# A fused attention and token-mixing kernel: a new static order of its instructions (measured durations, a reserve of buffers, PSUM emptied first, squares into later buffers, GpSimd products by chunks)

## The chip, the cores and the metric

The kernel runs on one core of one Trainium2 chip. A core has five engines that run at the same time, each through its own list of instructions in a fixed order: PE (TensorE, the matrix unit), DVE (VectorE), ACT (ScalarE), POOL (GpSimd) and SP (SyncE, which here only starts transfers). They wait for each other through semaphores. SBUF is the working memory, PSUM the eight banks into which PE writes; 128 partitions each.

The metric is the device time of one execution in microseconds (us), the median of several runs. The profile describes one further execution of the same program; its span, from the first to the last instruction, is a little shorter than the measured time.

## The reference

Two blocks follow each other. The first is an attention with a polynomial feature map; the second mixes tokens. There are 4 batches, 4 heads, 1088 positions, and 4 x 32 = 128 channels.

```python
def phi(x):                                   # r = 8 features from each of two sketches, 64 products
    a = einsum('rd,bhsd->bhsr', S1, x)
    b = einsum('rd,bhsd->bhsr', S2, x)
    return einsum('bhsi,bhsj->bhsij', a, b).reshape(..., r * r)
q_p, k_p = phi(q), phi(k)
kv  = einsum('bhsf,bhsd->bhfd', k_p, v)       # sums over all positions
z   = sum(k_p, axis=2)
num = einsum('bhsf,bhfd->bhsd', q_p, kv)
den = einsum('bhsf,bhf->bhs', q_p, z)[..., None] + 1e-06
x   = (num / den) as (batch, seq, 128)

theta = x @ w_theta
zr, zi = x * cos(theta), x * sin(theta)
y = einsum('ts,bsd->btd', w_tok_r, zr) + einsum('ts,bsd->btd', w_tok_i, zi)   # 1088 x 1088 each
u = x + y
return u + maximum(u @ w_ch, 0)
```

The token weights come in 64-bit floating point, so the kernel first makes 32-bit rows out of them. The denominator can come near zero, so it is computed with numbers split into a coarse and a fine part.

## The kernel before

The kernel doesn't write its instructions in the order in which they run. It records operations (`op`) with the engine, an estimated duration, and the buffers that they read and write. `Layout.run` then orders all of them when the program is built: it repeats "which ready operation can start first, and of those within a small slack, which is due first", keeps account of when engines and buffers come free, and fixes both the order on each engine and which buffer each value gets. On the chip nothing is decided any more.

```python
LAT = {"P": 0.16, "V": 0.12, "A": 0.12, "G": 0.16, "S": 0.10}
HURRY = 100.0
SLACK = {"P": 0.05, "V": 0.25, "A": 0.25, "G": 0.25, "S": 0.4}
...
def run(self):
    ... # due of an operation: the earliest due of those after it, less their duration and the latency
    for o in ops:
        if o.eng in "VA" and any(b.cls == "ps" for b in o.bufs):
            o.due -= self.HURRY                        # what empties PSUM goes first
    ...
    def place(o, strict=True):                         # is there room for the buffers of o, and from when
        ...
            k = len(bs) + (max(b.keep for b in bs) if strict else 0)
            if len(av) < k:
                return None
    ...
        t, o = min((c for c in cand if c[0] <= first + self.SLACK[e]), key=lambda c: (c[1].due, c[1].i))
...
classes = {"big": (24, 1152), "zs": (5, 2176), "lv": (1, 5 * NT), "hf": (2, 576), "g3": (4, 768),
           "g1": (4, 384), "sm": (12, 192), "ps": (5, 512), "py": (3, 512)}      # buffers, words each
```

The work, in the order of the data. "Row" is one of the 17 slices of the token weights (128 positions of the real or the imaginary part, the last one 64 of each).

```python
def weight(dst, dfn, src, n):                  # one 64-bit row into 32 bits
    raw = buf("zs", (n,), I64, "raw", cap=3)
    stp = buf("big", (n, 2), I16, "step", keep=0, cap=2)
    op("S", n * 1024 / 250e3, lambda: SY.dma_start(raw(), src), ...)
    op("A", 0.2 + n * 0.0009,  lambda: A.activation(dfn(), <high words>, AF.Copy, scale=2.0**-112), ...)
    op("A", 0.2 + n * 0.00105, lambda: A.activation(<step, upper half>, <high words>, AF.Copy, scale=2.0**-60), ...)
    op("A", 0.2 + n * 0.00105, lambda: A.activation(<step, lower half>, <low words>, AF.Copy, scale=2.0**-29), ...)
    op("V", n * 0.00095 + 0.05, lambda: ts(dfn(), dfn(), 3, ALU.logical_shift_left), ...)
    op("V", n * 0.0012 + 0.08, lambda: tt(V, dfn(), dfn(), stp(), ALU.add), ...)

def key_sums(b):                               # exact sums over the keys, for the denominator
    junk = buf("big", ...)
    op("A", ..., lambda: A.activation(junk(), kx(), AF.Square, accum_out=km()[:, 2:3]), ...)
    ...                                        # DVE: coarse part, rest, fine part
    op("G", pool_(n), lambda: tt(G, r(), r(), kb()[:, :, 1], ALU.subtract), [r], [(kb, 1)])
    tps = kfeatures(b)
    vop(n, lambda: stt(kc(), r(), -0.5, kc(), ALU.mult, ALU.add), [kx], [r])
    for c in range(NC):
        op("P", 0.4, lambda c=c: sums(c), [t], [kb, r, kx])      # 9 chunks
    ...

def kfeatures(b):                              # features of the keys, 3 groups, and k_p x v
    for g in range(NG):
        ...                                    # PE transposes, ACT, PE features, ACT
        op("G", pool_(CH * R * R), lambda: tt(G, kp(), <a>, <b>, ALU.mult), [kp], [ks])    # 128 x 768
        op("P", 1.0, sums, [acc], [kp, vx])

def chain(bs): ...                             # small matrices from the sums: PE and DVE by turns; for (0,) and (1, 2, 3)
def query_scale(b): ...                        # ACT squares of q into a "junk" buffer, PE, DVE
def query_slices(b): ...                       # PE transposes of q, ACT, DVE: coarse half and rest
def levels(b): ...                             # PE, ACT, then some 13 DVE operations: q features and 1/den

def outputs_x(b, lv, pool_qp):                 # 3 groups of 384 positions
    ...                                        # products q_p (DVE for batch 0, POOL for 1 to 3), PE transposes, ACT,
                                               # PE num, ACT, PE theta, ACT/DVE: cos and sin, DVE: z = x*cos, x*sin

def mix_row(b, i, gs, yps, due): ...           # PE: y += z[:, i] x row i; for batch 0 all three groups per row
def mix_out(b, g, yp, due): ...                # u, u @ w_ch, relu, out
...
due0, per = 40, 3.0
t = due0
for b in range(B):
    lv = levels(b)
    outputs_x(b, lv, b > 0)
    gss = ((0, 1, 2),) if b == 0 else tuple((g,) for g in range(NG))
    for gs in gss:
        for i in range(NK):
            t += per if b == 0 else 0.65
            mix_row(b, i, gs, yps, t)
        for g, yp in zip(gs, yps):
            mix_out(b, g, yp, t + 6.0)
```

Batch 0 is mixed row by row while the rows are still being made; batches 1 to 3 use all 17 finished rows, which stay in SBUF.

Of the kernel before, what the change touches and what calls it, by code (L numbers as in the profile page):

```python
# [21 lines left out]
P = 128  # L22
# [5 lines left out]
UP = 256.0  # L28
QFIX = 2.006
# [3 lines left out]
class Buf:  # L33


    def __init__(self, cls, shape, dt, name, keep=0, cap=99):
        self.cls, self.shape, self.dt, self.name, self.keep, self.cap = cls, shape, dt, name, keep, cap
        self.ops, self.left, self.slot, self.ap, self.end = [], 0, None, None, 0.0
# [5 lines left out]
class Op:  # L44
    __slots__ = ("eng", "dur", "fn", "bufs", "pred", "succ", "due", "wait", "ready", "start", "end", "i")


class Layout:
# [3 lines left out]
    HURRY = 100.0  # L52
    SLACK = {"P": 0.05, "V": 0.25, "A": 0.25, "G": 0.25, "S": 0.4}
# [5 lines left out]
    def buf(self, cls, shape, dt, name, keep=0, cap=99):  # L59
        return Buf(cls, shape, dt, name, keep, cap)  # L60

    def op(self, eng, dur, fn, w=(), r=(), due=None, hold=()):
        o = Op()
        o.i, o.eng, o.dur, o.fn, o.due = len(self.ops), eng, dur, fn, 1e9 if due is None else due
        o.succ, pred = [], set()
# [41 lines left out]
    def run(self):  # L107
        ops = self.ops
        for o in reversed(ops):
            for s in o.succ:  # L110
                t = ops[s]
                lat = 0.0 if t.eng == o.eng else self.LAT[o.eng]
                if o.eng == "S":
                    lat += 2.0
                o.due = min(o.due, t.due - t.dur - lat)
            o.wait, o.ready = len(o.pred), 0.0
        for o in ops:
            if o.eng in "VA" and any(b.cls == "ps" for b in o.bufs):
                o.due -= self.HURRY
# [6 lines left out]
        def place(o, strict=True):  # L126
# [5 lines left out]
            for c, bs in need.items():  # L132
                av = sorted(s[0] for s in slots[c] if s[1] is None)
                if any(sum(s[1] is not None and s[1].name == b.name for s in slots[c]) >= b.cap for b in bs):
                    return None
                k = len(bs) + (max(b.keep for b in bs) if strict else 0)
                if len(av) < k:
                    return None
# [3 lines left out]
        while done < len(ops):  # L142
            pick = None
            for e in "PVAGS":
                cand = []
                for o in ready[e]:
                    t = max(free[e], o.ready)
# [7 lines left out]
                t, o = min((c for c in cand if c[0] <= first + self.SLACK[e]), key=lambda c: (c[1].due, c[1].i))  # L155
                if pick is None or t < pick[0]:
                    pick = (t, o)
            if pick is None:
                loose = [(o.due, o.i, o) for e in "PVAGS" for o in ready[e] if place(o, False) is not None]
                if loose:  # L160
                    o = min(loose)[2]
                    pick = (max(free[o.eng], o.ready, place(o, False)), o)
            if pick is None:
                raise RuntimeError("no room: " + str([(o.eng, [b.name for b in o.bufs]) for e in "PVAGS" for o in ready[e]][:9]) + str({c: [x[1] and x[1].name for x in v] for c, v in slots.items()}))
            t, o = pick
            e = o.eng
            for b in o.bufs:
                if b.slot is None and b.cls is not None:
                    s = min((x for x in slots[b.cls] if x[1] is None), key=lambda x: x[0])
                    s[1], b.slot = b, s  # L170
            o.start = t
# [60 lines left out]
def pool_(n):  # L232
    return 0.06 + 0.0021 * n
# [3 lines left out]
def kernel(  # L237
# [30 lines left out]
        "hf": (2, 576),  # L268
        "g3": (4, 768),
# [86 lines left out]
    if wide:  # L356
# [24 lines left out]
        op("V", 1.1, unpack, [(sp, 0), y, z], [st])  # L381
# [52 lines left out]
    op("V", 1.2, scaled, [ab, sc, s0, sf, sq], [sp, pw])  # L434
# [89 lines left out]
    def weight(dst, dfn, src, n):  # L524
        if src.dtype == F32:
            op("S", n * 512 / 250e3, lambda: SY.dma_start(dfn(), src), [dst], [])
            return
        raw = buf("zs", (n,), I64, "raw", cap=3)
        stp = buf("big", (n, 2), I16, "step", keep=0, cap=2)
        op("S", n * 1024 / 250e3, lambda: SY.dma_start(raw(), src), [raw], [])  # L530
        op("A", 0.2 + n * 0.0009, lambda: A.activation(dfn(), words_of(raw(), n)[1].bitcast(F32), AF.Copy,  # L531
                                                     scale=2.0**-112), [dst], [raw])
        op("A", 0.2 + n * 0.00105, lambda: A.activation(stp()[:, :, 1].bitcast(F16), words_of(raw(), n)[1].bitcast(F32),  # L533
                                                     AF.Copy, scale=2.0**-60), [(stp, 1)], [raw])
        op("A", 0.2 + n * 0.00105, lambda: A.activation(stp()[:, :, 0], words_of(raw(), n)[0].bitcast(U32), AF.Copy,  # L535
                                                     scale=2.0**-29), [(stp, 0)], [raw])
        op("V", n * 0.00095 + 0.05, lambda: ts(dfn().bitcast(I32), dfn().bitcast(I32), 3, ALU.logical_shift_left),
           [dst], [])
        op("V", n * 0.0012 + 0.08, lambda: tt(V, dfn().bitcast(I32), dfn().bitcast(I32),
                                          stp().rearrange("p n t -> p (n t)").bitcast(I32), ALU.add), [dst], [stp])  # L540
# [4 lines left out]
    def load(b, nm, due=None):  # L545
        src = {"k": k, "q": q, "v": v}[nm]
        t = ld[nm, b] = buf("big", (NC, H, D), F32, f"{nm}{b}", keep=5)
        op("S", 576 * 1024 / 250e3, lambda: SY.dma_start(t().rearrange("p c h d -> p (c h d)"),
                                                        src[b].rearrange("p c h d -> p (c h d)")), [t], [], due)
# [4 lines left out]
    def key_sums(b):  # L554
# [6 lines left out]
        junk = buf("big", (NC * HD,), F32, "junk")  # L561
        op("A", act(n) + 0.1, lambda: A.activation(junk(), kx().rearrange("p c h d -> p (c h d)"), AF.Square,
                                                   accum_out=km()[:, 2:3]), [junk, (km, 1)], [kx])
        kg[b] = fixed((2,), F32, f"kg{b}")
        pg = buf("ps", (512,), F32, "pg", keep=2 * (b > 0))
# [14 lines left out]
        vop(n, lambda: rnd(kb()[:, :, 0], kc(), km()[:, 0:1]), [(kb, 0)], [kx, (km, 0)])  # L580
        vop(n, lambda: tt(V, r(), kc(), kb()[:, :, 0], ALU.subtract), [r], [kx, (kb, 0)])
        vop(n, lambda: rnd(kb()[:, :, 1], r(), km()[:, 1:2]), [(kb, 1)], [r, (km, 0)])
        op("G", pool_(n), lambda: tt(G, r(), r(), kb()[:, :, 1], ALU.subtract), [r], [(kb, 1)])
        tps = kfeatures(b)
        vop(n, lambda: stt(kc(), r(), -0.5, kc(), ALU.mult, ALU.add), [kx], [r])
# [457 lines left out]
```

## Time and profile before

| what | value |
|---|---|
| time, median of 3 runs (lowest, highest) | 298.12 us (297.23, 298.13) |
| span of the profiled execution, and its own time | 292.5 us, 294.28 us |
| PE busy | 253.1 us, 87% of the span |
| DVE busy | 166.6 us, 57% |
| ACT busy | 143.3 us, 49% |
| POOL busy | 61.2 us, 21% |
| read from and written to memory | 26.30 MB and 2.23 MB |

In the profile a line of a group names the line of the program, the engine, the operation, the buffers written and read by their class (`big`, `zs`, `ps` and so on, as in `classes` above) and the shape. Matmuls into `py` are the token mixing; a 32-bit matmul shows as two records. A busy engine can be held up inside an instruction: the length of one instruction against the usual length of its group tells that. Busy time is listed for PE as records that overlap, so it is best read beside the work itself.

### The profile page before, as it was taken

What the parts mean: (1) busy time and instruction counts of PE and PEld (TensorE: products, weight loads), DVE (VectorE), ACT (ScalarE), POOL (GpSimd) and SP (SyncE); (2) the same over time, 40 slices, a digit from 0 to 9 for tenths busy, and PEclk for the clock granted to TensorE, in tenths of its full rate; (3) what the DMA queues carried; (4) which work ended last, traced back from release to release, by engine and by line L of the source; (5) the groups of instructions that cost most, each with busy time, mean ns of one, the idle gap of its engine ahead of it and who ended that gap; (6) DMA issues with size and microseconds to landing.
All of it is one profiled execution on the core that took longest, in us unless ns stands there. A gap on an engine that the chain in (4) does not pass through costs nothing.

```text
span 292.5 us, 3825 instructions
## 1 busy us (share of the span) xinstructions
PE 253.1 (87%) x1447; PEld 183.3 (63%) x1447; DVE 166.6 (57%) x343; ACT 143.3 (49%) x231; POOL 61.2 (21%) x67
## 2 busy tenths in 40 slices
PE   2329969677979999999199999999999999999993
PEld 2329859454557878867067667676657676666671
DVE  2998787998996966799985304813400721501001
ACT  5454945869886988999048202037300235500000
POOL 0328912502371307200270000140000060000000
PEclk9999968979999999999689999999999999999999
DMA  6999910040564457620001101000001010000000
GB/s 214 411 417 420 415 46 3 0 152 2 173 262 160 147 195 272 205 117 2 0 0 30 51 0 29 0 27 0 2 22 27 0 29 0 0 25 7 20 27 24
DMA packets 9155, 28.77 MB, mean 98 GB/s; under 512 B 945, under 2 KB 5297, under 8 KB 6961
## 3 DMA queue, kind: packets, MB, share of 16 engines
q1 hardware_dynamic: 9136, 28.53, 26.7%
q8 instruction: 11, 0.18, 0.2%
q14 instruction: 8, 0.06, 0.1%
HBM read 26.30 MB, written 2.23 MB: 98 GB/s over the span
## 4 chain that ended last, share of the span: by engine, by line
PE 64%; DVE 17%; ACT 11%; DMA 4%; issue 3%; SPq 0%; DVEq 0%; ACTq 0%
PE py L311 37%; PE ps L311 22%; DVE big L295 4%; DMA zs<-w_tok 3%; ACT big L531 3%; DVE lv L295 3%; ACT big L533 2%; ACT big L535 2%; DVE big L299 2%; PE ps L863 2%; DVE big L302 1%; DMA big<-k_l 1%; DVE g L295 1%; PE ps L948 1%; DVE sm L295 1%
## 5 line engine op out<-in xcount | busy, mean ns | idle before, releaser
L311 PE MATMUL py<-big,zs 128*128 128x384 f32 (+1 forms) x408 | 137.1, 477 | 8.4 <-DVE big L295 7.1
L311 PEld LDWEIGHTS py<-big,zs 128*128 128x128 f32 x408 | 73.8, 192 | 50.5 <-DVE big L295 8.9
L958 ACT ACTIVATE g<-ps 128x384 f32<-128x384 f32 (+2 forms) x16 | 6.1, 406 | 77.0 <-PE ps L311 77.0
L295 POOL TENSOR_TENSOR g<-lv 128x768 f32<-128x768 f32 x9 | 15.9, 1789 | 100.5 <-DVE lv L295 100.5
L295 POOL TENSOR_TENSOR g<-sm 128x768 f32<-128x768 f32 x12 | 24.5, 2045 | 39.9 <-ACT sm L630 29.2
L295 DVE CUSTOM_DVE_ANT_0 big<-big,big 128x2176 uint16<-128x2176 uint16 x17 | 24.3, 1430 | 6.5 <-ACT big L535 5.8
L533 ACT ACTIVATE big<-zs 128x1088 f16<-128x1088 f32 (+1 forms) x18 | 24.8, 1380 | 0.0
L535 ACT ACTIVATE big<-zs 128x1088 int16<-128x1088 uint32 (+1 forms) x18 | 24.7, 1372 | 0.0
L295 DVE TENSOR_TENSOR g<-big,py 128x384 f32<-128x384 f32 (+1 forms) x12 | 6.2, 527 | 31.1 <-PE py L311 31.1
L295 DVE TENSOR_TENSOR g<-g,ps 128x384 f32<-128x384 f32 (+2 forms) x16 | 6.9, 450 | 26.4 <-PE ps L948 19.3
L531 ACT ACTIVATE big<-zs 128x1088 f32<-128x1088 f32 x17 | 20.4, 1201 | 0.0
L302 DVE SCALAR_TENSOR_TENSOR g<-g,ps 128x384 f32<-128x384 f32 x12 | 6.6, 553 | 22.4 <-ACT g L893 22.4
L311 PE MATMUL ps<-big,big 128*128 128x128 f32 x72 | 16.8, 317 | 1.2 <-DVE big L302 1.2
L867 ACT COPY g<-ps 128x384 f32<-128x384 f32 x24 | 10.4, 488 | 14.9 <-PE ps L863 14.8
L299 DVE TENSOR_SCALAR big<-big 128x1088 int32<-128x1088 int32 x17 | 17.0, 1003 | 1.3 <-ACT big L531 1.3
L295 POOL TENSOR_TENSOR big<-big,big 128x1152 f32<-128x1152 f32 x4 | 10.4, 2608 | 31.1 <-DVE big L299 26.9
L311 PE MATMUL ps<-mf,big 128*128 128x96 f32 x72 | 16.0, 320 | 0.0
L295 DVE TENSOR_TENSOR zs<-ps,g 128x768 f32<-128x768 f32 (+2 forms) x20 | 12.3, 629 | 3.3 <-ACT g L899 3.3
L863 PE MATMUL ps<-ident,g 128*128 128x128 f32 x72 | 11.1, 299 | 3.4 <-DVE sm L299 3.4
L311 PE MATMUL ps<-mv,hf 128*128 128x96 f16 x108 | 12.0, 218 | 2.0 <-DVE mv L299 1.1
L863 PEld LDWEIGHTS ps<-ident,g 128*128 128x128 f32 x72 | 9.2, 154 | 6.2 <-issue 4.8
L311 PEld LDWEIGHTS ps<-big,big 128*128 128x128 f32 x72 | 11.6, 202 | 2.1 <-DVE big L302 1.6
(159 smaller groups left out, 393.9 us busy)
## 6 DMA issues: line engine op xcount, KB each, us to landing
zs<-w_tok SPq DMA_DIRECT2D x17, 1088.0 KB, 5.0
big<-k_l SPq DMA_DIRECT2D x4, 576.0 KB, 10.1
big<-q_l SPq DMA_DIRECT2D x4, 576.0 KB, 12.6
big<-v_l SPq DMA_DIRECT2D x4, 576.0 KB, 12.9
out<-g SPq DMA_DIRECT2D x8, 192.0 KB, 2.1
out<-g SPq DMA_DIRECT2D x4, 128.0 KB, 1.8
zs<-w_sq SPq DMA_DIRECT2D x1, 256.0 KB, 4.9
out<-g SPq DMA_DIRECT2D x4, 32.0 KB, 1.8
```

The lines of the kernel that those rows point to most:

```text
L295: eng.tensor_tensor(out=o, in0=a, in1=b, op=f)
L299: (eng or V).tensor_scalar(out=o, in0=a, scalar1=s1, scalar2=s2, op0=op0, **kw)
L302: (eng or V).scalar_tensor_tensor(out=o, in0=a, scalar=s, in1=b, op0=op0, op1=op1)
L311: T.matmul(o, lhs, rhs, start=start, stop=stop, skip_group_check=True)
L531: op("A", 0.2 + n * 0.0009, lambda: A.activation(dfn(), words_of(raw(), n)[1].bitcast(F32), AF.Copy, scale=2.0**-112), [dst], [raw])
L533: op("A", 0.2 + n * 0.00105, lambda: A.activation(stp()[:, :, 1].bitcast(F16), words_of(raw(), n)[1].bitcast(F32), AF.Copy, scale=2.0**-60 ...
L535: op("A", 0.2 + n * 0.00105, lambda: A.activation(stp()[:, :, 0], words_of(raw(), n)[0].bitcast(U32), AF.Copy, scale=2.0**-29), [(stp, 0)] ...
L863: T.transpose(tr()[:, i * P:(i + 1) * P], qp()[:, i * H + 2 * n:i * H + 2 * n + 2].rearrange("p h i j -> p (h i j)"), ident())
L867: op("A", act(GW), lambda n=n, tr=tr, qT=qT: A.copy(qT()[:, n], tr()), [(qT, n)], [tr])
L948: T.transpose(un()[:sz, i * P:(i + 1) * P], uT()[:, i * P:i * P + sz], ident())
L958: op("A", act(m), lambda n=n, i0=i0, i1=i1, o=o: A.activation(o(), po()[:n, i0 * P:i1 * P], AF.Relu), [(ot, j)], [po])
```

## The change

The order on all engines is made anew. Nothing of the arithmetic changes: each engine executes the same operations as before, except that each large POOL product is now three smaller ones. The parts:

- **Durations of the trace.** The estimates given to `op` are replaced by lengths that a trace showed (for instance small DVE chains 2.5 us instead of 1.1, feature matmuls 0.615 instead of 0.67, loads at 380 to 400 GB/s instead of 250).
- **A reserve of buffers for what is due first.** The fixed `keep` and `cap` of each buffer go. A buffer that is due later may only be taken while enough free ones remain for those due earlier, up to `RESERVE` of its class.
- **PSUM emptied first.** The 100 us of hurry for what empties PSUM now changes only the choice among ready operations (`rank`), no longer the due time (`due`), which the reserve and the new lead times use.
- **Squares into later buffers.** The squares that only serve their sum are written where a later value will stand (`kb`, `qx`), not into a buffer of their own; the half-corrected keys get their own buffer `kh`, so the keys aren't overwritten.
- **POOL products by chunks.** Each product of 128x768 becomes three of 128x256, each difference of 128x1152 three of 128x384.
- **Due times and lead times.** Rows are due at 55.2 + 2.18 i us of the layout's own clock, mixing at 54.7 + 2.05 per row; loads of q, k and v may start at most 40 us ahead of their due time. One more buffer in `hf` and `g3`.

```diff
+MIX = (54.7, 2.05, 0.691, 0.0)
+ROWS = (55.2, 2.18)
+LOAD_LEAD = 40.0
+RAW_LEAD = 1000.0
+CHAINS = ((0,), (1, 2, 3))
+QPOOL = (False, True, True, True)
...
+    RESERVE = {"big": 8, "zs": 2, "lv": 0, "hf": 1, "g3": 3, "g1": 2, "sm": 4, "ps": 3, "py": 0}
...
-            o.wait, o.ready = len(o.pred), 0.0
+            o.wait, o.ready, o.rank = len(o.pred), 0.0, o.due
         for o in ops:
             if o.eng in "VA" and any(b.cls == "ps" for b in o.bufs):
-                o.due -= self.HURRY
+                o.rank -= self.HURRY
...
-                k = len(bs) + (max(b.keep for b in bs) if strict else 0)
-                if len(av) < k:
+                last = max((b.due, b.ops[0]) for b in bs)
+                before = bisect.bisect_left(pending[c], last, key=lambda x: x[:2]) - len(bs) + 1
+                if len(av) < len(bs) + min(max(before, 0), self.RESERVE[c]):
                     return None
...
-                    t = max(free[e], o.ready)
+                    t = max(free[e], o.ready, o.due - o.lead)
...
-        "hf": (2, 576),
-        "g3": (4, 768),
+        "hf": (3, 576),
+        "g3": (5, 768),
...
-        junk = buf("big", (NC * HD,), F32, "junk")
-        op("A", act(n) + 0.1, lambda: A.activation(junk(), kx()..., AF.Square, accum_out=km()[:, 2:3]), [junk, (km, 1)], [kx])
+        op("A", act(n) + 0.1, lambda: A.activation(kb()[:, :, 0], kx()..., AF.Square, accum_out=km()[:, 2:3]), [(kb, 0), (km, 1)], [kx])
...
-        op("G", pool_(n), lambda: tt(G, r(), r(), kb()[:, :, 1], ALU.subtract), [r], [(kb, 1)])
+        def rest():
+            for g in range(NG):
+                x = r()[:, g * GC:(g + 1) * GC]
+                tt(G, x, x, kb()[:, g * GC:(g + 1) * GC, 1], ALU.subtract)
+
+        op("G", pool_(n) + 0.1, rest, [r], [(kb, 1)])
         tps = kfeatures(b)
-        vop(n, lambda: stt(kc(), r(), -0.5, kc(), ALU.mult, ALU.add), [kx], [r])
+        kh = buf("big", (NC, HD), F32, "kh")
+        vop(n, lambda: stt(kh(), r(), -0.5, kc(), ALU.mult, ALU.add), [kh], [r, kx])
...
+            def outer(kp=kp, ks=ks):
+                for i in range(GC):
+                    h = slice(i * H, (i + 1) * H)
+                    tt(G, kp()[:, h], bc(ks()[:, h, 0:R], ...), bc(ks()[:, h, R:2 * R], ...), ALU.mult)
...
-    due0, per = 40, 3.0
-    t = due0
+    t = MIX[0]
...
-                t += per if b == 0 else 0.65
+                t += MIX[1] if b == 0 else MIX[2]
...
-                mix_out(b, g, yp, t + 6.0)
+                mix_out(b, g, yp, t + 6.0 + (3.0 * g if b == 0 else 0.0))
```

## Prediction

> **What bounds the kernel now.** I began with the page's picture of 40 slices (7.3 us each, busy share in tenths), to see in which stretches PE has holes.
>
> ```profile
> PE   2329969677979999999199999999999999999993
> ...
> DVE  2998787998996966799985304813400721501001
> ACT  5454945869886988999048202037300235500000
> POOL 0328912502371307200270000140000060000000
> ```
>
> PE is sparse to slice 8 and has one hole in slice 19; after it PE is full to the end while DVE and ACT are half idle. So there are stages. I cut the trace at the first transposes of query products (60 us), at the end of batch 0's mixing (149) and at the last matmul (288.2), and asked for busy time in each stretch (PE, weight loads, DVE, ACT, POOL, then clock, DMA share, GB/s):
>
> ```profile
> 0.00:60.00 60.00, 38.03 (x287) 33.95 (x287) 47.68 (x142) 35.06 (x60) 24.60 (x49) 0.94 0.62 242
> 60.00:149.00 89.00, 77.00 (x485) 56.76 (x486) 75.89 (x116) 70.09 (x86) 25.27 (x12) 0.94 0.37 134
> 149.00:288.20 139.20, 138.06 (x678) 92.56 (x675) 42.41 (x85) 38.04 (x85) 11.29 (x7) 1.00 0.06 16
> 288.20:292.50 4.30, 0.00 (x0) 0.00 (x0) 0.61 (x2) 0.06 (x1) 0.00 (x0) 0.91 0.15 40
> ```
>
> The third stage is PE alone, 138.06 of 139.2 us. The second has PE, DVE and ACT all at 79 to 87%: no engine is full, they wait for each other. The waits of PE name the largest of these:
>
> ```profile
> PE py L311 <- DVE big L295: 7.1, 3, 6.1
> PE ps L393 <- DVE m L411: 5.9, 1, 5.9
> PE ps L619 <- DMA big<-k_l: 4.7, 1, 4.7
> PE ps L863 <- DVE sm L299: 3.4, 1, 3.4
> PE ps L311 <- DVE psc L495: 3.2, 1, 3.2
> ```
>
> The 6.1 us is the hole in slice 19: the last weight row waits on DVE, which has the whole levels chain of batch 1 (138.0 to 144.2 us) ahead of the row's last step. The others lie in the first 21 us and before batch 0's products. Last, why DVE is slow there; the timeline of DVE, then of POOL, in one window:
>
> ```profile
> 78.02 0.71 DVE L299 TENSOR_SCALAR big<-big 128x1088 int32<-128x1088 int32 x1
> ...
> 81.23 2.90 DVE L299 TENSOR_SCALAR big<-big 128x1088 int32<-128x1088 int32 x1
> ```
>
> ```profile
> 80.24 3.31 POOL L295 TENSOR_TENSOR big<-big,big 128x1152 f32<-128x1152 f32 x1 [4.16 <-issue]
> ```
>
> The same shift takes 0.71 us alone and 2.90 us when POOL has begun a long difference just before; it ends as soon as POOL has (83.55).
>
> [...]2.2 us lost in one hold. Other such excesses over the usual length in the second stage: 1.9 (74.05 us), 1.3 (85.33), 1.3 (97.97), 1.2 (114.40), 1.3 and 1.2 (145.38, 147.48): about 10 us with the 2.2. [...]Here a 128x32 product takes 0.21 us and an undisturbed 128x768 one 1.48, which makes 1.73 ns per element and 0.155 us fixed[...]. [...]a chunk of the levels matmuls takes 0.75 us at 42 us and 0.39 from 46 us; the row at 145.5, behind the hole, takes 3.50 instead of 1.9.[...]
>
> **The yardstick.** All PE work, by start-to-start spacings where PE is dense: mixing 136 x 0.645 + 68 x 0.54 = 124.4; 220 transposes x 0.11 = 24.2; levels 36 x 0.39 = 14.0; key sums 36 x 0.445 = 16.0; key features 36 x 0.205 = 7.4; k_p v 72 x 0.134 = 9.6; num 24 x 0.40 = 9.6; theta and the last product 72 x 0.222 = 16.0; folding 16 x 0.22 = 3.5; small ones 6.1. Sum 230.8 us. The change leaves it as it is; it can only alter how much is lost beside it. Before, the work done at the two cuts is 26.6 and 96.2, so the stages lost 60 - 26.6 = 33.4, 89 - 69.6 = 19.4 and 139.2 - 134.6 = 4.6 us.
>
> **First stage.** From the recorded order of the changed kernel, walked by hand with the old trace's lengths:
> - The five small sketch loads now go before k. Five issues at about 0.45 us put k about 2.3 us later: landing 6.9 instead of 4.5. That is a loss. In exchange DVE unpacks the sketches while it waits for k, not after it behind a 2.36 us hold.
> - Coarse and fine parts of k on DVE end near 13.0 (before 11.8), POOL's rest near 15.5. The sketch scaling starts at 16.0 (18.2 before) and ends 17.7. The half-corrected keys follow at once, 17.7 to 19.0; before they came after all small pieces, 24.0 to 26.4, also held by POOL.
> - So batch 0's key sums start at 19.0 instead of 26.15. From there to the end of the levels matmuls the old kernel took 21.3 us; I give the new one 24, because two k_p v sums stand ahead of the levels on PE and wait for POOL products, and DVE takes q's rest (1.35) only after the small chain. The levels end at 43, not 47.5.
> - From the levels to the first query transposes: 12.6 us before, of which some 3.6 were POOL holds (this DVE chain takes 9.8 us in batch 0, 6.2 in batch 1). I take 10.5.
> Together 53.5 us instead of 60. PE has done 24.3 of its work by then, 2.3 less than before.
>
> **Second stage.** PE has 96.1 - 24.3 = 71.8 us to do. The three other limits, summed along the new order with the old durations less their 0.08 to 0.11 us overlap: ACT from the first copies of query products to the last row's conversion 65.4 us; DVE from there to the last row's addition 66.6 us (16 shifts at 0.64, 17 additions at 1.22, levels 6.2, chain 4.65, and so on), with perhaps 6 of holds 73. PE, ACT and DVE would be done within 8 us of each other, so PE leads narrowly. What is new in the order: the 27 key-sum chunks of batches 1 to 3 (12 us) lie around the first mixed rows, where PE used to wait for z and rows, and the levels chain of batch 1 comes when the seventeenth row is five rows away. The 6.1 us hole and its 1.6 us of slow clock go. I take 71.8, 2.5 of overhead as in the dense stage (4.6 / 134.6), 3 of slow clock after the thin start, 3 of waits: 80 instead of 89.
>
> **Third stage and end.** The same instructions, 134.7 + 4.6 = 139.3, and 4.3 for the last copies and transfer, which aren't touched.
>
> **Chunks alone.** Each product costs 2 x 0.155 = 0.31 us more on POOL, 25 of them some 8 us: POOL from 61 to about 69 busy, nearly all beside other work. A hold can last 0.6 to 0.8 us instead of 1.5 to 2.4.
>
> **Sum.** 53.5 + 80 + 139.3 + 4.3 = 277 span. The measured time before is 5.6 above its profiled span (298.12 - 292.5): 283 us, 5% less.
>
> **Rivals.** (1) *DVE or ACT takes over in the second stage.* For it: three engines within 8 us, in-order lists, so each late value stalls what stands behind; the old stage lost 12 us of PE this way at about the same load. Against it: the hole had one named cause, which is gone. Then stage two stays at 86 to 89 and the time is 289 to 292. (2) *The first stage gains nothing*: k lands later, and the POOL products ahead of the levels are waited for. Then 60 + 78: about 288. (3) *The loads come too late*: q and v of batches 1 to 3 now load one by one between the rows, and ACT would stop at their squares. Against it: a row lands in 5.0 us and memory is 37% busy in that stage; q of batch 3 is needed well after batch 0's end. If one stalls PE by 5 us: 288. (4) *Better than I think*: stage two at its PE floor of 74 and the start at 51 make 275.
>
> **Range and chances.** The third stage is fixed to 1 or 2 us, so the spread is that of the first (plus or minus 4) and second (minus 5, plus 9). Mostly independent, that gives 272 to 292 for 8 in 10. Two per cent faster is 292.2, which only rivals (1) and (2) together miss: 0.87 faster, 0.08 the same, 0.05 slower, the last for a stall that I have not seen.
>
> **What would show it.** First query transposes near 53 us, with key sums starting near 19; the last row of batch 0 mixed near 134, without a DVE wait of several us before it; from there to the last matmul 139 us with PE at 99%[...]; POOL busy near 69. I am wrong if the stage of batch 0 is still over 86 us, or if PE has idle stretches after it.

## The result and the profile after

The changed kernel takes 285.42 us (median of 4 runs, 284.84 to 285.87), the kernel before beside it 297.68 (294.68 to 298.13): a ratio of 0.961, with a 95% interval of 0.954 to 0.968. A second set of rounds gave 285.39 and 0.961 (0.954 to 0.967). The prediction was 283, range 272 to 292.

The page's picture of the changed kernel, 40 slices of 7.1 us each:

```profile
PE   0539699686999999949999999999999999999993
...
DVE  3686898996998989999452338124052612401001
ACT  2993834798589899894880310373022036400000
POOL 0079061569003137829100000701000340000000
```

PE is still thin up to slice 9, and there is still one hole, now in slice 17 instead of 19 and half as deep. DVE is busy for 80% or more of every slice from 4 to 18 but slice 9. The same cuts as before the change (first transposes of query products, end of batch 0's mixing, last matmul) give this table; the columns are those of the prediction's table:

```profile
0.00:56.20 56.20, 36.38 (x251) 32.23 (x251) 42.64 (x132) 34.42 (x58) 23.10 (x60) 0.91 0.64 253
56.20:140.10 83.90, 76.53 (x497) 56.95 (x498) 75.29 (x121) 70.11 (x89) 39.44 (x36) 0.96 0.39 139
140.10:279.20 139.10, 138.33 (x699) 92.80 (x698) 43.34 (x90) 38.66 (x84) 12.46 (x21) 1.00 0.07 20
279.20:283.50 4.30, 0.38 (x3) 0.11 (x2) 0.61 (x2) 0.48 (x2) 0.00 (x0) 0.71 0.14 38
```

The first stage fell from 60 to 56.2 us, the second from 89 to 83.9, the others stayed. So 3.8 + 5.1 us were gained; predicted were 6.5 + 9. DVE's busy time in the second stage hardly fell (75.9 to 75.3 us): it now fills 90% of that stage. What PE waited for (in total, times, the longest):

```profile
PE ps L635 <- DMA big<-k_l: 7.1, 1, 7.1
PE ps L321 <- DVE big L312: 5.3, 3, 3.0
PE py L321 <- DVE big L305: 3.9, 1, 3.9
PE ps L403 <- DVE m L421: 3.3, 1, 3.3
PE ps L321 <- DVE sm L309: 2.7, 2, 1.4
```

The third line is the old hole (6.1 us before), now ahead of the thirteenth row. The second is the wait for half-corrected keys: 3.0 us before batch 0's key sums and 2.2 in those of batch 1. Last, DVE's own timeline at two places (start, length, engine, line, operation, output<-inputs):

```profile
36.90 0.54 DVE L309 TENSOR_SCALAR mv<-sm 128x32 f16<-128x32 f32 x1
37.48 0.56 DVE L305 TENSOR_TENSOR sm<-sm,mv 128x32 f32<-128x32 f32 x1
38.07 0.55 DVE L312 SCALAR_TENSOR_TENSOR sm<-sm,sm 128x32 f32<-128x32 f32 x1
...
108.75 1.72 DVE L305 CUSTOM_DVE_ANT_0 big<-big,big 128x2176 uint16<-128x2176 uint16 x1
110.39 1.14 DVE L309 TENSOR_SCALAR big<-big 128x1088 int32<-128x1088 int32 x1
...
120.56 0.71 DVE L309 TENSOR_SCALAR big<-big 128x1088 int32<-128x1088 int32 x1
122.96 1.28 DVE L305 CUSTOM_DVE_ANT_0 big<-big,big 128x2176 uint16<-128x2176 uint16 x1
```

and POOL's beside it:

```profile
108.01 11.34 POOL L305 TENSOR_TENSOR g<-sm 128x256 f32<-128x256 f32 x9 [5.93 <-PE ps L321]
```

At 120 us, with POOL quiet, a row's shift takes 0.71 and its addition 1.28 us; at 109 us, while POOL works through nine chunks, they take 1.14 and 1.72. The small steps of the chain at 37 us take 0.55 instead of 0.18, one to each POOL chunk. So a chunk holds a DVE operation for 0.2 to 0.44 us here (a shift 0.43, an addition up to 0.44, a small step 0.37), and while POOL has a backlog that comes again at nearly every operation of DVE: the eight from 108.75 to 118.9 us are all longer by that much than their like beside a quiet POOL.

Before the runs there were two readings of the gain. **T**: the new order gains, the chunks give next to nothing. **C**: the shorter holds gain. And two of what is left: **H**, POOL's holds cost it in both places seen above; against it for the hole **O**, the order of DVE's list alone.

### The profile page after: what moved, and what is told of

It is laid out like the page before. It is cut to its first block, busy times and chain, and to the rows that moved or that the text cites. A ratio compares the mean times of both kernels' runs of the same rounds, so it can differ in the third digit from the quotient of the medians.

```text
span 283.5 us, 3868 instructions
## 1 busy us (share of the span) xinstructions
PE 251.6 (89%) x1447; PEld 182.1 (64%) x1447; DVE 161.9 (57%) x343; ACT 143.7 (51%) x231; POOL 75.0 (26%) x117
## 4 chain that ended last, share of the span: by engine, by line
PE 74%; DVE 17%; issue 2%; POOL 2%; ACT 2%; DMA 1%; SPq 1%; DVEq 0%; ACTq 0%
PE py L321 41%; PE ps L321 26%; DVE big L305 3%; DVE big L309 3%; PE ps L887 2%; DVE lv L305 2%; DVE big L312 2%; POOL big L305 2%; DVE sm L305 1%; PE ps L635 1%; PE ps L972 1%; DMA big<-k_l 1%; PE ps L908 1%; DVE sm L309 1%; PE ps L805 1%
## 5 line engine op out<-in xcount | busy, mean ns | idle before, releaser
L305 POOL TENSOR_TENSOR g<-sm 128x256 f32<-128x256 f32 x36 | 30.3, 874 | 52.4 <-DVE zs L305 21.5
L305 POOL TENSOR_TENSOR g<-lv 128x256 f32<-128x256 f32 x27 | 20.1, 778 | 82.1 <-DVE lv L305 79.9
L543 ACT ACTIVATE big<-zs 128x1088 f16<-128x1088 f32 (+1 forms) x18 | 24.8, 1379 | 0.7 <-DVE big L312 0.7
L321 PE MATMUL ps<-big,big 128*128 128x128 f32 x72 | 19.0, 352 | 5.3 <-DVE big L312 5.3
L305 POOL TENSOR_TENSOR big<-big,big 128x384 f32<-128x384 f32 x12 | 14.9, 1276 | 17.9 <-DVE m L421 12.8
L321 PEld LDWEIGHTS ps<-big,big 128*128 128x128 f32 x72 | 13.3, 230 | 7.0 <-DVE big L312 6.1
L309 DVE TENSOR_SCALAR big<-big 128x1088 int32<-128x1088 int32 x17 | 14.3, 843 | 0.0
L321 PE MATMUL ps<-mf,big 128*128 128x96 f32 x72 | 14.2, 295 | 0.0
L808 ACT ACTIVATE big<-ps,qs 128x384 f32<-128x384 f32 x12 | 6.1, 572 | 15.4 <-PE ps L805 10.7
L321 PE MATMUL ps<-big 128*128 128x256 bf16 x72 | 13.9, 281 | 0.0
L831 ACT COPY lv<-ps 128x480 f32<-128x480 f32 x12 | 5.9, 567 | 15.1 <-PE ps L321 15.0
```

The lines of the kernel that those rows point to most:

```text
L305: eng.tensor_tensor(out=o, in0=a, in1=b, op=f)
L309: (eng or V).tensor_scalar(out=o, in0=a, scalar1=s1, scalar2=s2, op0=op0, **kw)
L321: T.matmul(o, lhs, rhs, start=start, stop=stop, skip_group_check=True)
L543: op("A", 0.24 + n * 0.00105, lambda: A.activation(stp()[:, :, 1].bitcast(F16), words_of(raw(), n)[1].bitcast(F32), AF.Copy, scale=2.0**-6 ...
L808: op("A", act(GW) + 0.1, lambda g=g, tr=tr: A.activation(f()[:, g * GW:(g + 1) * GW], tr(), AF.Copy, scale=s()[:, 0:1]), [(f, g)], [tr, (s ...
L831: op("A", act(480), lambda g=g, lp=lp: A.copy(lv().rearrange("p l (c n) -> p l c n", n=HR)[:, :, g * GC:(g + 1) * GC], lp().rearrange("p c ...
```

## The experiments

The edits were measured in several rounds, each with the kernel before beside them. That kernel had medians from 294.98 to 297.68 us and single executions from 293.88 to 299.06; the changed kernel lay between 284.84 and 285.87 in both of its sets. Gains of 2 to 3 us on the changed kernel are taken against its 285.4 us from other rounds. As a ratio to the kernel before they don't show (0.959 and 0.961 for two of them, 0.961 for the changed kernel itself), so they rest on the traces as well.

### Order and chunks apart

Whole products in the new order (every engine's order otherwise that of the changed kernel):

```diff
-            for g in range(NG):
-                x = r()[:, g * GC:(g + 1) * GC]
-                tt(G, x, x, kb()[:, g * GC:(g + 1) * GC, 1], ALU.subtract)
+            tt(G, r(), r(), kb()[:, :, 1], ALU.subtract)
 ...                                    # the key and query products likewise
```

> The changed kernel with whole POOL products, every engine's order as in the changed kernel. Theory T (the new order gains, the chunks give nearly nothing, because POOL with a backlog takes DVE's next gap again): 284 to 288 us, POOL busy near 67 instead of 75; single DVE operations are held up to 2.3 us instead of 0.5 to 1, but fewer of them. Rival C (the shorter holds gain): 291 us or more, with the first mixed rows and the hole at 120 us back at 6 us.

And chunks in the old order, the same edit the other way round in the kernel before.

> The kernel before with POOL products by chunks, every engine's order as before. Theory T: 295 to 299 us, within 1% of the kernel before; the 6 us hole of PE before the last weight row stays, since it comes from the levels chain standing first on DVE. Rival C: 291 us or less and the hole under 3 us.

Measured: whole products in the new order 289.47 us (289.35 to 291.81), 0.979 of before (0.972 to 0.986). Chunks in the old order 294.4 us, 0.994 (0.987 to 1.001). So T's numbers failed by 1.5 us (whole products) and 0.6 us (chunks in the old order), and C's failed too: the order alone brings 2.1%, the chunks alone 0.6% or nothing (the interval holds 1), and in the new order the chunks bring a further 4 us (289.5 to 285.4). PE's waits for weight rows in the old order with chunks, and then in the new order without:

```profile
PE py L311 <- DVE big L295: 7.4, 3, 6.1
```

```profile
PE py L321 <- DVE big L305: 5.7, 3, 2.8
```

In the old order the 6.1 us stay, as T said: the levels chain stands ahead of the row whatever POOL does. In the new order without chunks 5.7 us are spread over three waits, with chunks it is one of 3.9. That is 1.8 of the 4 us. PE itself is busy for another 2.7 us, 254.3 without chunks and 251.6 with them, for the same work: before 75 us its granted clock is at half for some 20 us in the traced execution without chunks (34.0 to 44.2, 57.9 to 68.1) and for 13.7 in the one with them. Whether the holds bring that about too was not tried. What chunks cost and save there, by the group of key products (with chunks it is 36 instructions of 0.874 us, 30.3 in all):

```profile
L305 POOL TENSOR_TENSOR g<-sm 128x768 f32<-128x768 f32 x12 | 21.9, 1835 | 59.4 <-DVE zs L305 26.4 <-ACT sm L644 16.7 <-PE ps L321 16.3
```

POOL as a whole is busy 56.5 us without chunks (T expected 67) and 75.0 with them, while DVE is busy 167.7 without and 161.9 with. Here the shorter instructions made DVE 5.8 us less busy and POOL 18.5 us more, and POOL has time (busy for 26% of the span).

### The hole at 120 us

The key products of batches 1 to 3 left out (their buffers filled with zeros by POOL, which reads nothing), all orders kept:

```diff
+                if b > 0:
+                    G.memset(kp(), 0.0)
+                    return
                 for i in range(GC):
                     ...                # three chunks
```

> The changed kernel, the POOL products of the key features of batches 1 to 3 left out (each replaced by one filling of the same buffer with zeros, which reads nothing), order kept. Theory H (POOL's chunks hold DVE at 108 to 119 us, and that is what opens the 3.9 us hole of PE at 120 us): the hole is under 1.5 us, the second stage 80 to 81 us instead of 83.9, the time 281 to 282.5. Rival O (the levels chain of batch 1 stands ahead of the row's addition on DVE, whatever POOL does): hole still 3 us or more, time 284 or more.

Measured 280.6 us (280.3 to 280.9), 4.8 less than the changed kernel. The wait behind the hole is nearly gone:

```profile
PE py L321 <- DVE big L305: 0.8, 1, 0.8
```

DVE's busy time fell from 161.9 to 156.9 us with all its own work kept, so these nine products hold DVE for 5.0 us in all, close to the 4.8 us gained; 3.6 of them lie in the second stage, which takes 80.6 instead of 83.9 us. 1.7 us of the gain lie before the first query transposes (54.5 instead of 56.2), where the same products held batch 0's levels chain. H holds, O falls. Whether an earlier row alone would also do was still open, so the thirteenth row's shift and addition were moved ahead of the fifth operation of batch 1's levels chain:

```diff
     L.run()
+    mine = [o for o in L.order if o.eng == "V" and any(x.name == "w12" for x in o.bufs)]
+    for o in mine:
+        L.order.remove(o)
+    L.order[i:i] = mine                # i: ahead of the fifth operation of the chain, or where ACT is done
```

> The changed kernel with the thirteenth row's two DVE steps moved ahead of five operations of batch 1's levels chain, nothing else moved. Rival O (only the order of DVE's list makes the 3.9 us hole): the hole is gone, the next rows are not later, 281.5 to 283 us. Theory H (DVE is short of time from 108 to 136 us because POOL holds it, so an earlier row makes others later): the hole before this row shrinks by 1.5 to 3 us, one of nearly that length opens before the next row, and the time stays within 1 us of 285.4.

Measured 286.38 us (286.1 to 286.6), no gain. PE's timeline of that kernel, the thirteenth and fourteenth row:

```profile
122.62 2.10 PE L321 MATMUL py<-big,zs 128*128 128x384 f32 x6 [1.65 <-DVE big L305]
...
128.08 2.10 PE L321 MATMUL py<-big,zs 128*128 128x384 f32 x6 [2.71 <-DVE big L305]
```

The row's addition came 1.7 us earlier (121.28 instead of 122.96 us), the wait before it shrank from 3.9 to 1.65 us and one of 2.7 opened before the next row: 4.4 together. A third, of 0.9 us, opened at the query products, which stand behind the levels chain. DVE has no time to spare there, and this move only passed the wait on. It is the one place that was tried.

### The first stage

Batch 0's key products left out in the same way, so that POOL would not alternate with the small chain at 35 to 40 us:

```diff
+                if b == 0:
+                    G.memset(kp(), 0.0)
+                    return
```

> The changed kernel, the POOL products of the key features of batch 0 left out (zeros instead), order kept. Theory H (POOL's nine chunks alternate with the small DVE operations at 35 to 40 us, 0.55 us each instead of 0.18): these go back to 0.2 us or less, the levels matmuls of batch 0 begin near 38.5 instead of 42.65, the time is 281 to 283. Rival D (the small operations are long because each waits for the one before it, or the gain is lost again before the first rows): the operations stay over 0.4 us, or levels earlier but the time 284.5 or more.

Measured 287.55 us, 2 us *slower* than with the products. The first half of H was right. DVE's timeline:

```profile
37.33 0.18 DVE L309 TENSOR_SCALAR mv<-sm 128x32 f16<-128x32 f32 x1
37.54 0.19 DVE L305 TENSOR_TENSOR sm<-sm,mv 128x32 f32<-128x32 f32 x1
```

The steps are short again and the chain ends at 38.5 us instead of 40.4, although it began 1.2 us later (one DVE step of 0.34 us took 1.34 while the zeros were written, 28.08 to 30.17 us). But the levels came at 44.3 us, 1.7 later than in the changed kernel. PE's timeline of this kernel, ahead of them:

```profile
39.91 1.55 PE L321 MATMUL ps<-g,big 128*64 128x128 f32 x12
41.38 1.54 PE L635 MATMUL ps<-ident,big 128*128 128x128 f32 x6
42.85 1.55 PE L321 MATMUL ps<-g,big 128*64 128x128 f32 x12
44.34 0.42 PE L321 MATMUL ps<-mv,hf 128*128 128x96 f16 x3
```

PE has no wait from 34.3 us to the levels; it works at half clock, here until 45.6 us. Twelve k_p v matmuls take 1.55 us and at full clock 0.88 (48.54 us). The same holds in the changed kernel, without a wait from 33 us to the levels at 42.65. Its granted clock (the column after PE's busy time):

```profile
32.00:40.00 8.00, 8.00 (x44) 0.50 0.66 250
```

So the held chain that I had taken for the cause was hidden behind a slow PE: D, in a form I had not thought of. PE is slow once more ahead of that, in the key sums, where a chunk takes 0.85 us up to 24.8 us and 0.45 from there on. The changed kernel's timeline of PE:

```profile
23.11 0.53 PE L321 MATMUL ps<-big 128*128 128x256 bf16 x2
23.43 0.74 PE L321 MATMUL ps<-big,big 128*128 128x128 f32 x2
23.97 0.53 PE L321 MATMUL ps<-big 128*128 128x256 bf16 x2
...
25.37 0.33 PE L321 MATMUL ps<-big 128*128 128x256 bf16 x2
25.54 0.44 PE L321 MATMUL ps<-big,big 128*128 128x128 f32 x2
25.81 0.33 PE L321 MATMUL ps<-big 128*128 128x256 bf16 x2
```

To test it, PE's waits between 11 and 32 us were filled, since slow matmuls stand behind waits in the changed kernel's trace (the first six chunks of the key sums behind one of 2.95 us; the thirteenth row, 3.63 us instead of 1.99, behind 3.9):

```diff
+    def fill(n, at):                   # n transposes of the identity into a bank that nobody reads
+        def f():
+            for _ in range(n):
+                T.transpose(spare()[:, :P], ident(), ident())
+        ...                            # placed in PE's list ahead of operation "at"
+    fill(24, <max of the sketches>), fill(10, <its second step>), fill(24, <key sums>),
+    fill(10, <first step of the chain>), fill(11, <its second step>)
```

> The changed kernel; PE's waits between 11 and 32 us are filled with 79 extra transposes of the identity into a bank that nobody reads, so that its clock does not fall. Theory P (PE at half clock, 0.50 in 32 to 40 us, and not DVE's held chain, makes the levels late): the chunks of the key sums take 0.45 instead of 0.85 us each from the first, the sums end near 24 instead of 26.4, the levels matmuls begin near 38.5 to 39.5 instead of 42.65, the time is 280.5 to 282.5. Rival V (the chain on DVE, alternating with POOL, then binds at the old place): levels at 41.5 or later, the time 284 or more.

Measured 282.88 us (282.33 to 285.91). PE's timeline:

```profile
20.02 0.49 PE L321 MATMUL ps<-big,big 128*128 128x128 f32 x2 [0.56 <-DVE big L312]
...
23.98 0.43 PE L321 MATMUL ps<-psc,sx 8*128 8x64 f32 x2
...
39.81 0.42 PE L321 MATMUL ps<-mv,hf 128*128 128x96 f16 x3
```

The key sums end at 24.0 instead of 26.4 and the levels begin at 39.8 instead of 42.65. That is P, a little short of its numbers (38.5 to 39.5; 280.5 to 282.5), and not where P had put it: 2.4 of the 2.8 us were won in the key sums. From their end to the levels it still takes 15.8 us (16.3), since the clock fell again at 34 us (it reads 0.50 from there to 40.9), in the middle of dense work, and PE then waited 1.1 us for DVE. So the slow sums are shown to cost 2.4 us; what the half clock from 32 us on costs was not taken away and is not shown. The gain of 2.5 us came with 79 matmuls *more*. Neither the drop to half clock nor the return goes with one length of waiting or of work here. The drop came in the changed kernel with two waits of 1.25 and 1.33 us (28.6 to 31.8 us), and in this one with no wait over 0.54 us in the 6 us before it. The return took 3.4 us of work after the last wait in this kernel (37.5 to 40.9 us), but 10.2 us without any wait in the changed one (31.9 to 42.1).

The other term of the first stage is the landing of the keys. The order of loads only:

```diff
     L.run()
+    s = [o for o in L.order if o.eng == "S"]
+    L.order.remove(s[1])                           # the first keys
+    L.order.insert(L.order.index(s[0]), s[1])      # ahead of the sketches
```

> The changed kernel, the first keys loaded ahead of the five small sketch loads (as before the change), all other orders kept. Theory K (the keys set the start: squares, sums and coarse parts follow their landing): keys land at 4.7 us instead of 7.0, the key sums start near 17.9 instead of 19.97, the time falls by about 2 to 283 to 284. Rival S (the sketches' unpacking and scaling set the start, or the gain is lost before the first rows): key sums at 19.5 or later, or the time 285 or more.

Measured 283.28 us (282.79 to 284.2). PE's timeline:

```profile
4.69 2.15 PE L635 MATMUL ps<-ident,big 128*128 128x128 f32 x9 [4.69 <-DMA big<-k_l]
...
18.13 0.79 PE L321 MATMUL ps<-big,big 128*128 128x128 f32 x2 [2.96 <-DVE big L312]
...
53.79 0.85 PE L887 MATMUL ps<-ident,g 128*128 128x128 f32 x6 [1.45 <-DVE g L305]
```

K holds: keys 2.4 us earlier, sums 1.8, first query transposes 2.4, time 2.1. The new order's loads (sketches first) are a loss, as the prediction counted it.

### The parts of the layout

The kernel before with only the new durations and due times:

```diff
-            op("V", 1.1, unpack, ...)                   # and some twenty estimates like it
+            op("V", 2.5, unpack, ...)
-    due0, per = 40, 3.0
+    due0, per = 54.7, 2.05                              # rows due at 55.2 + 2.18 i
```

> The kernel before with two parts of the change alone: the new durations and the new due times of rows and mixing (whole products, squares in own buffers, fixed keeps and caps). Rival D (better numbers alone make the better order): 287 to 290 us, about what the changed order has with whole products (289.5). Theory R (without the reserve the early rows take the buffers of what is due first): the first stage 60 us or more and the time 292 or more.

Measured 289.55 us, 0.980 of before (0.970 to 0.990): D's number, and that of the changed order with whole products. The way there is another, with R's mark on it (a first stage of 60 us or more). PE's timeline:

```profile
66.97 1.49 PE L863 MATMUL ps<-ident,g 128*128 128x128 f32 x6
...
131.38 5.50 PE L311 MATMUL py<-big,zs 128*128 128x384 f32 x12 [5.00 <-DVE big L295]
```

The first stage is 67 us, 7 longer than before, the hole is still 5.0 us, and batch 0's last row ends at 155.1 us, 6 later than before. The gain comes after it: 133 us to the end instead of 143.5, because PE has done more of the other batches' work by then. And the changed kernel with all reserves at 0:

```diff
-    RESERVE = {"big": 8, "zs": 2, "lv": 0, "hf": 1, "g3": 3, "g1": 2, "sm": 4, "ps": 3, "py": 0}
+    RESERVE = {"big": 0, "zs": 0, "lv": 0, "hf": 0, "g3": 0, "g1": 0, "sm": 0, "ps": 0, "py": 0}
```

> The changed kernel laid out without any reserve of buffers (all reserves 0), all other parts of the change kept. Theory R (the reserve keeps the early rows and loads from taking what batch 0's products and batch 1's keys need first): rows start or finish later, 291 to 298 us, nearly the whole gain lost. Rival N (durations, due times and chunks suffice; the reserve is a detail): within 2 us of 285.4.

Measured 302.66 us, 1.021 of before (1.012 to 1.031), worse than R expected. PE's timeline:

```profile
93.57 1.99 PE L321 MATMUL py<-big,zs 128*128 128x384 f32 x6
...
110.55 0.90 PE L908 MATMUL ps<-ident,big 128*128 128x128 f32 x3 [5.12 <-DVE g L312]
...
114.07 3.83 PE L321 MATMUL py<-big,zs 128*128 128x384 f32 x6
```

Between the third and the fourth row of batch 0 lie 20 us, in which the outputs of batch 0's second group are made: on DVE five row steps (101.2 to 109.9 us) stand ahead of the operation that the group waits for. So the reserve isn't a gain on top: it replaces the old keeps and caps, and without either the better numbers are worth nothing. The squares into later buffers, the emptying of PSUM and the lead times of the loads were not tried by themselves.

### A version that beats both

The idea was that POOL's holds cost DVE about as much as the products themselves would. Then DVE may as well do them whole, where they are quicker (a 128x768 product takes 0.96 us on DVE, three POOL chunks 1.9 undisturbed and 2.6 on average). And what DVE lacks in the second stage it has in the third. So:

```diff
-CHAINS = ((0,), (1, 2, 3))
+CHAINS = ((0,), (1, 2), (3,))
-QPOOL = (False, True, True, True)
+QPOOL = (False, False, False, False)
-        op("G", pool_(n) + 0.1, rest, [r], [(kb, 1)])
+        vop(n, lambda: tt(V, r(), r(), kb()[:, :, 1], ALU.subtract), [r], [(kb, 1)])
-            op("G", pool_(CH * R * R) + 0.1, outer, [kp], [ks])        # stays so for batch 0
+            vop(CH * R * R, <the product whole, on DVE>, [kp], [ks])
...                                    # due times, slack and reserve adapted
```

> A try at a better version, laid out anew: the large POOL products go to DVE as whole operations (keys' rests 128x1152, key products of batches 1 to 3 and query products 128x768; only batch 0's key products stay on POOL by chunks), and batch 3's chain is separate from that of batches 1 and 2, so that its key work can leave the second stage; due times and reserve adapted. Theory H (POOL's holds cost DVE as much as the work itself would, and the second stage is bound by DVE): 273 to 279 us, key sums from near 16 us, the last row of batch 0 before 130 us, no hole over 3 us, while DVE is busier by 10 us or more outside the second stage. Rival L (DVE is the bound and gets 20 to 25 us more work of its own): 286 us or more, with longer waits of PE on DVE in the second stage.

Measured 283.2 us (282.0 to 285.2), between H and L. The table by stages of this version, with the same cuts, says which part of H held:

```profile
0.00:54.74 54.74, 36.82 (x233) 32.90 (x234) 42.28 (x133) 38.56 (x58) 17.44 (x51) 0.86 0.74 285
54.74:128.90 74.16, 71.19 (x440) 52.68 (x441) 66.48 (x111) 66.26 (x90) 0.00 (x0) 0.97 0.35 130
128.90:275.70 146.80, 146.22 (x784) 99.58 (x784) 63.75 (x132) 38.43 (x84) 0.00 (x0) 1.00 0.08 23
```

The second stage is what H expected: last row before 130 us, no wait of PE over 1.3, PE busy 96% of the stage. DVE is busier by 11 us in all (173.1 against 161.9 us): by 20 in the third stage, where it has time, and less by 9 in the second. (The key sums start at 17.1 us, expected near 16.) H's premise fails, though. One group of the products on DVE:

```profile
L305 DVE TENSOR_TENSOR g<-sm 128x768 f32<-128x768 f32 x9 | 8.6, 951 | 1.6 <-PE ps L886 1.6
```

With the nine query products (8.6 us) and the four rests (5.4) that is 22.6 us of work moved to DVE, which became busier by 11.2; so the holds that went were some 11.4 us, an estimate from these figures (eleven operations more for the separate chain are left out of it). The products cost DVE nearly twice what POOL's holds did; for the nine key products alone it is 8.6 against 5.0 us. What relieves DVE in the second stage is that batch 3's key work left it, too. The two were not run apart, so what moving the products gains by itself is not shown. And of the 9.7 us by which the second stage is shorter, 7.7 come back as batch 3's key work in the third, which PE must do somewhere. Only PE's waits and slow clock can be gained, and I had put too much of them into the second stage: in the first, PE is idle for 18 of 55 us, and its clock is at half from 29 to 39 us and again from 50 to 56. So the two aids for the first stage were added:

```diff
+    L.order.insert(L.order.index(s[0]), s[1])           # the first keys ahead of the sketches
+    fill(30, <key sums>), fill(14, <first step of the chain>),
+    fill(3, ...), fill(6, ...), fill(6, ...)            # batch 1's first transposes and key features
```

> The version with the large products on DVE and batch 3's chain apart, and in addition the two things that shortened the first stage by themselves: the first keys loaded ahead of the sketches, and 59 extra transposes into an unused bank in PE's waits before 50 us. Theory A (they act on different waits and add up, since all that is left to lose lies in the first stage): 277 to 280 us, first query transposes near 51 us. Rival B (keys that land earlier and a faster PE end in the same wait on DVE or POOL): 281 us or more.

The changed kernel beside it, unedited:

> The changed kernel itself once more, beside the version with everything, so that the two are compared in the same rounds: 284.5 to 286.5 us.

Measured in the same rounds: 274.88 us for the version with everything and 285.39 for the changed kernel, against 296.02 before: 0.926 (0.918 to 0.933) and 0.961. From its page, busy times and PE's picture:

```profile
PE 257.5 (93%) x1514; PEld 189.1 (68%) x1514; DVE 173.3 (63%) x376; ACT 143.1 (52%) x231; POOL 17.4 (6%) x51
...
PE   3979799799999996999999999999999999999993
```

A holds, with more than it promised (277 to 280): 8.3 us less than without the two, where each had given 2.1 and 2.5. Why more than their sum is not shown: the one execution with a trace took 278.38 us, the four others 274.76 to 275.05, and in the traced one the first query transposes came at 53.1 us, only 1.6 earlier than without. Its clock was at half from 28.8 to 45.8 us in spite of the fillings. On record the mean granted clock is 0.966 for it and 0.983 for the four others, which makes (an estimate) 19 us at half clock against 9, if the clock is either half or full, as the changed kernel's column has it up to 75 us (in windows of 0.5 us it reads 0.50 or 1.00 but for those at the edges). But the changed kernel took 285.55 and 285.40 us at 0.954 and 285.39 at 0.966, so the mean clock alone doesn't settle it.

## Why the prediction was right, and where it was not

The time is inside the range and 2.4 us above the middle. By its own steps:

- **Sum.** Two errors met. The span was to be 277 us and is 283.5, 6.5 too low. The measured time was to lie 5.6 above the span, and lies 1.7 above it (285.24 for the profiled execution). The 5.6 came from setting a profiled execution of 294.28 us against a median of 298.12 from others; against its own time the difference was 1.8. With that the prediction would have been 279: the mechanism stands, the closeness of 283 is partly luck.
- **First stage, 53.5; measured 56.2.** Keys landed at 7.0 (6.9), the key sums could start at 19.97 (19.0): right to a microsecond. From there to the end of the levels I gave 24 us; it took 26.3. This is the step that failed. I had looked for its excess in the k_p v sums, waiting for POOL products, and in DVE; PE waited for no POOL product there. The runs showed half a clock on PE: six of the nine chunks of the key sums (before the change three) at 0.85 us instead of 0.45, which is 2.4 us (levels 2.8 us earlier once PE was kept busy, no earlier when DVE's chain was freed). The old stretch was no safe measure either. From the start of the sums to that of the levels it took 14.9 us before (26.15 to 41.07) and takes 22.7 now: moved forward, the sums have the 18 key-feature matmuls behind them (33.1 to 37.4 us, at half clock), which before came ahead of them (21.7 to 26.1). That the levels now take 3.6 us at nearly full clock instead of 6.3 hides part of it. From the levels to the query transposes it took 10.0 (10.5).
- **Second stage, 80; measured 83.9.** "The 6.1 us hole and its 1.6 us of slow clock go" failed: 3.9 us stayed, with 1.7 of slow clock (the row takes 3.63 instead of 1.99). In the sum, the term "3 of waits" was mis-sized: PE's waits in the stage are 1.1 + 0.2 + 2.2 + 3.9 = 7.4 us. That is rival 1, DVE taking over, in part: it was argued away with "the hole had one named cause, which is gone". The cause named, the levels chain in front of the last row, no longer stands there. It stands in front of the thirteenth, and moving that row ahead of a part of it gained nothing: beneath lay DVE's want of time, at least 3.6 us of it spent in POOL's holds.
- **Third stage and end, 139.3 + 4.3; measured 139.1 + 4.3.** Right.
- **Chunks alone.** "0.31 us more POOL each", 8 us in all, was far too little: 18.5 us (56.5 to 75.0) in the new order, 16.4 (61.2 to 77.6) in the old one. A chunk is longer when long DVE operations run beside it: nine take 11.34 us at 108 us, beside rows and levels, 5.30 at 35 us, beside the small chain, and 5.31 at 224 us, with DVE nearly idle. Undisturbed, a chunk takes 0.62 us (batch 0's nine, with the other key products left out), the average one of the key products 0.87. The holds stayed short, as foreseen: the longest shift took 1.15 us, 0.43 over its usual 0.72, where a hold of 0.6 to 0.8 was allowed for. A reading of the old trace was off here: the held shift did not end as soon as POOL had (83.55 us) but at 84.13, 0.6 us later, about what it takes alone.
- **Rivals.** Rival 2 was wrong for the sum (the first stage gained 3.8 us) and half right about what it would meet: k lands later, but PE waits for no POOL product. Rival 3 did not come: PE's only wait for a load is the one for the first keys.

## What to carry to other kernels

Where one engine's long instructions hold another's, cutting them into pieces can shorten each hold much more than their sum: here the longest held shift fell from 2.90 us in the kernel before to 1.15 in the changed one, DVE's whole busy time, in the same order, only from 167.7 to 161.9. Before the work is moved to the engine that is held, compare what the holds cost it with what the work would (here some 11 us, an estimate, with 22.6): the move was tried only together with one that took other work to a stage with time to spare. Read an engine's delay together with what the next engine in the chain was doing meanwhile: the most conspicuous slow row (a chain at three times its length) cost nothing that the runs could find, because PE behind it was slower still. And take the difference between profiled span and time from one and the same execution.

## What was not expected of the hardware

- POOL's chunks and DVE's small operations take turns: with a backlog on POOL, DVE gets one small operation per chunk, 0.55 us instead of 0.18 (36.9 to 39.7 us; one starts every 0.58 us, and nine chunks take 5.30, 0.59 each). What lies behind these turns, and behind the holds, was not shown.
- In the filled kernel PE fell to half clock at 34 us in dense work, with no wait over 0.54 us in the 6 us before (from 29.5 us on small matmuls, 64 columns wide and less). What it was that the clock answered to stays open. By the clock column, stretches at half clock before 75 us lasted 3.4 and 10.2 us in the changed kernel (from 69.4 and 31.9 us), 6.8 in the filled one (from 34.0), 13.7 without batch 0's key products (from 31.9) and 17.1 in the fastest version (from 28.8). What sets their length is open, too.
- The clock column isn't a safe witness by itself here: in the changed kernel it reads 1.00 from 20 to 24 us while a chunk of the key sums takes 0.85 us, and from 24.8 us on, with the same reading, 0.45. In the run without batch 0's key products equal chunks of 0.85 us stand under a reading of 0.50. In these runs the spacing of equal matmuls told more.
